# A fused decay attention and mixture of experts: GpSimd decays the next chunk's queries right behind the recall, ahead of the decay of the state

## The chip, the cores and the metric

One core of one Trainium2 chip runs the kernel. The metric is the device time of one execution in microseconds (us); less is better. The engines are TensorE (PE, with its weight loads as PEld), VectorE (DVE), ScalarE (ACT), GpSimd (POOL) and SyncE (SP), which here issues nearly all transfers between HBM and SBUF.

## What is computed

For 4 sequences of 768 positions, 8 heads and head size 64, all in float32, an attention with decay and no softmax, in blocks of 64 positions:

```
intra = einsum('bhic,bhjc->bhij', qb, kb) * Dmask      # lam ** (i - j), 0 above the diagonal
intra = einsum('bhij,bhjd->bhid', intra, vb)
inter = einsum('bhid,bhde->bhie', qb * lam_pow, kv_state)
out[block] = intra + inter
kv_state = lam_block * kv_state + einsum('bhsd,bhse->bhde', kb * rev_pow, vb)
```

The output, as 3072 rows of 512, goes through a soft mixture of 8 experts with 4 slots each: logits `x @ phi`, a softmax over all rows that fills the 32 slots, two matrix products per expert with a relu between them, and a softmax over the slots that hands the result back to the rows.

## The kernel before

The kernel takes blocks of 128 positions instead of 64, which gives 6 chunks for each sequence and T = 24 chunks in all, numbered t = 0 to 23. A chunk holds all 8 heads, two to each of four pairs. The loop over the chunks (from line 532 on) does the attention of one chunk a turn and, every four chunks, a step of the softmax over the rows. Behind the loop come the experts: the two products with w1 and w2, and the rows of the output. The weights are loaded all along, between the chunks' queries, keys and values.

Every engine runs its instructions in the order in which the program issues them: the helper class `InOrder` (its line 63 is the one that all rows of the profile name) keeps that order on each engine. So the order of the calls in the loop is the order of each engine's queue. The parts of a turn that matter here are these.

- `scores(t)`: PE multiplies keys and queries into two PSUM banks (tile sc). In chunks 0 and 1 and in every fourth chunk the scores are made whole, in the others the blocks above the diagonal are left out. `masks(t)`: DVE multiplies them with the powers of lam (tile at).
- `recall(t)`: PE multiplies the state st with the decayed queries qs of this chunk into the banks xa and xb. A chunk that opens a sequence (t = 0, 6, 12, 18) has no recall.
- `attend(t)`: PE adds the product of at and the values to the same banks, the half xa first, then xb; ACT copies them to xt.
- `state(t)`: PE multiplies the decayed keys kd and the values (bank kv), and DVE adds the decayed old state dec to make the new st. In odd chunks and in those that open a sequence this comes right behind the recall, ahead of `attend(t)`; in the other even chunks behind `attend(t)`. The last chunk of a sequence has none.
- POOL's part are three multiplications: `decay_q(t)` makes qs from the loaded queries and the powers qpow (128x512), `decay_k(t)` makes kd from the keys (128x512; in odd chunks from kn, the keys that PE turned and ACT copied), `decay_state(t)` makes dec from st (128x256). Each of qs, kd and dec has one buffer: the next qs can be written only when the recall that reads the old one is done. In chunk 2 POOL also copies phi and blk.
- In even chunks PE also turns the next chunk's keys (tile kv from ident and ld) and two finished chunks (tr, dp) behind the recall.

`decay_q(t + 1)` stands behind `attend(t)`. So in odd chunks and in those that open a sequence POOL's queue reads dec of chunk t, qs of chunk t + 1, kd of chunk t + 1; in the other even chunks it reads qs of t + 1, kd of t + 1, dec of t. No DMA is issued by POOL.

Of the kernel before, what the change touches and what calls it, by code (L numbers as in the profile page):

```python
# [68 lines left out]
def decay_attn_soft_moe(  # L69
# [23 lines left out]
    def bank(tag):  # L93
        return ps.tile([P, 512], F32, tag=tag, name=tag)
# [10 lines left out]
    def load_chunk(t, which=(0, 1, 2, 3)):  # L105
        srcs = (qT, kT, vN, kN)
        for i in which:
            if i == 3 and not loaded(t):
                continue
            tl = loads.tile([P, 512], F32, tag="ld", name="ld")  # L110
            sp.dma_start(out=tl, in_=srcs[i][t])
            IN[t, i] = tl
# [15 lines left out]
    def load_one(pool_, tag, bufs, n=1):  # L128

        t_ = pool_.tile([P, n, 512], F32, tag=tag, name="w2t", bufs=bufs)  # L130
        for m in range(n):
            Q, x, q, i = single.pop()
            sp.dma_start(out=t_[:, m], in_=rows(Q, x, q)[i])
            wt["w2", Q, q, x, i] = t_[:, m]
# [27 lines left out]
    def load_early(n):  # L162
        for _ in range(n):
            if early:
                Q, kk, q = early.pop()
                t_ = slabs.tile([P, 2, 1024], F32, tag="slab", name="slab")
                src = w1[4 * Q + q].rearrange("k p n f -> (k p n f)").rearrange("(p n y) -> n p y", p=P, n=2)
                sp.dma_start(out=t_.rearrange("p i f -> p (i f)"), in_=src[kk])
                wt["w1", Q, q, kk] = t_
            else:  # L170
                load_two()
# [83 lines left out]
    def scores(t):  # L255
        q_, k_ = IN[t, 0], IN[t, 1]
        if t < 2:
            SC["banks"] = [bank(x) for x in (("gl", "dp") if t == 0 else ("sc0", "sc1"))]
        banks = SC["banks"]

        if whole(t):
            for hp in range(HP):
                for hh in range(2):
                    r = slice(64 * hh, 64 * hh + 64)
                    pe.matmul(
                        out=banks[hh][:, hp * P:(hp + 1) * P],
                        lhsT=k_[r, hp * P:(hp + 1) * P],
                        rhs=q_[r, hp * P:(hp + 1) * P],
                        start=True,
                        stop=True,  # L270
                    )
            SC[t] = banks
            return
        for hp in (0, 2, 1, 3):
            for col in (1, 0):

                j = col if plain(hp) else 1 - col
                x = hp * P + 64 * j
                for hh in range(2):
                    r = slice(64 * hh, 64 * hh + 64)  # L280
                    pe.matmul(
                        out=banks[hh][64 * col:64 * col + 64, x:(hp + 1) * P],
                        lhsT=k_[r, hp * P + 64 * j:hp * P + 64 * j + 64],
                        rhs=q_[r, x:(hp + 1) * P],
                        start=True,
                        stop=True,
                    )
        SC[t] = banks
# [15 lines left out]
    def decay_q(t):  # L304
        if t < T and t % NB > 0:
            qs = work.tile([P, HP, P], F32, tag="qs", name="qs")
            pool.tensor_tensor(out=qs, in0=IN[t, 0].rearrange("p (a b) -> p a b", a=HP), in1=qpow, op=ALU.mult)
            QS[t] = qs

    def turn_k(t, tag="kv"):  # L310

        if t < T and t % NB < NB - 1 and not loaded(t):
            tk = bank(tag)
            for hp in range(HP):
                pe.transpose(tk[:, hp * P:(hp + 1) * P], IN[t, 1][:, hp * P:(hp + 1) * P], ident)
            kn = work.tile([P, D], F32, tag="kn", name="kn")
            act.copy(out=kn, in_=tk)
            IN[t, 3] = kn
# [15 lines left out]
    def place(t, hh, hp):  # L334

        g, a = divmod(hp, 2)
        return XB[t][hh][64 * a:64 * a + 64, g * P:(g + 1) * P]

    def recall(t):
        XB[t] = [bank("xa"), bank("xb")]  # L340
        if t % NB > 0:

            qs, st = QS.pop(t), ST["st"]
            for hp in range(HP):
                for hh in range(2):
                    r = slice(64 * hh, 64 * hh + 64)
                    pe.matmul(
                        out=place(t, hh, hp),
                        lhsT=st[r, hp, :],
                        rhs=qs[r, hp, :],  # L350
                        start=(hp < 2),
                        stop=True,
                        skip_group_check=True,
                    )
# [177 lines left out]
    for t in range(T):  # L532
        if t + 2 < T:
            load_chunk(t + 2, (0, 1))

        want = min(NSLAB, max(0, (t * PACE + AHEAD) // 100))
        load_early(want - sent)
        sent = max(sent, want)
        if t + 2 < T:
            load_chunk(t + 2, (2, 3))  # L540
        if t == 0:
            sp.dma_start(out=L, in_=phi.rearrange("p a s -> p (a s)"))

        for _ in range((2, 4, 3)[t - T + 3] if t >= T - 3 else 0):
            load_one(*ld1)
        if t == T - 1:
            load_one(work, "kd", 1)
            load_one(work, "kn", 1)
        last = t == T - 1

        asks = t // 4 - 1 if t > 0 and t % 4 == 0 else G - 1 if last else None
        sums = t // 4 - 1 if t > 4 and t % 4 == 1 else None
        if t == 0:
            turn_k(0, "tr")
            scores(0)
            scores(1)
            turn_v(0)
        elif t > 1:
            scores(t)
        masks(t)  # L560
        if last:
            ask = logits(asks)
            next(ask)

        if t % 4 == 3 or t % 4 == 0:
            next(sm, None)
        if t == T - 1:
            next(sm, None)
        opens = t % NB == 0
        if t == 0:  # L570
            decay_k(0)
            decay_q(1)
        recall(t)
        if sums is not None:
            sm = slot_softmax(sums, weights())
        if t % 2 == 0 and t > 0:
            turn_k(t + 1)
            natural(t - 2)
            natural(t - 1, "dp")
        if sums is not None:  # L580
            next(sm)
        if asks is not None and not last:
            ask = logits(asks)
            next(ask)
        if last:
            natural(t - 1)
            next(ask)
            weights(raw=False)

            phi4 = work.tile([P, HP, 4, SL], F32, tag="carry", name="phi4")  # L590
            four = phi_sb.rearrange("p (a o) s -> p a o s", o=1)
            pool.tensor_copy(out=phi4, in_=four.broadcast_to([P, HP, 4, SL]))
        if opens or t % 2 == 1:

            state(t)
            decay_state(t)
            if t == 0:
                turn_k(1, "tr")
        attend(t)
        if last:  # L600
            cm = bank("kv")
            pe.matmul(out=cm[:, 0:4], lhsT=blk_, rhs=gm, start=True, stop=True)
            dve.tensor_reduce(out=own, in_=cm[:, 0:4], axis=AX.X, op=ALU.min)
        if t == 1:
            powers_of(range(HP, HP + 2), d)
            dve.tensor_reduce(out=sel, in_=ident.rearrange("p (g s) -> p s g", g=4), axis=AX.X, op=ALU.add)
            for n in range(4):
                own_ = bass.AP(
                    tensor=ident.tensor,
                    offset=ident.offset + 16 * (n // 2) + NR * (n % 2),  # L610
                    ap=[ident.ap[0], [64, 2], [40, 2], [1, NR]],
                )
                dve.tensor_reduce(out=own4[:, n:n + 1], in_=own_, axis=AX.XYZ, op=ALU.add)
            dve.tensor_reduce(out=gsel, in_=ident.rearrange("p (g s) -> p g s", g=4), axis=AX.X, op=ALU.add)
        if t > 0:
            decay_q(t + 1)
        if not opens and t % 2 == 0:
            state(t)
        decay_k(t + 1)
        if not opens and t % 2 == 0:  # L620
            decay_state(t)
        if asks is not None and not last:
            next(ask)
        if sums is not None:
            slots(sums)
        if t == 2:
            place_phi()
        if t == 2:
            pool.tensor_copy(out=blk, in_=sel.rearrange("p (o s) -> p o s", o=1).broadcast_to([P, 4, SL]))
# [309 lines left out]
```

## Time and profile before

| | |
|---|---|
| time, median of 3 runs | 169.1 us (168.83 to 170.04) |
| the profiled execution | 169.32 us, its span 167.5 us |
| PE busy | 144.2 us (86%) |
| PEld, DVE, ACT, POOL busy | 104.3, 88.9, 69.1, 70.8 us |
| SP's DMA queue | 61.68 MB, 97.0% of 16 engines' span |
| moved over the span | mean 370 GB/s |

Times in the profile are counted from the start of the span. The chunk loop lies in about the first 113 us, the experts and the output behind it. A row of a timeline gives start, duration, engine, operation, output <- inputs, shapes, and in brackets how long the engine was idle ahead of it and what ended that. PE's matmuls are pipelined and their ends are modelled, so starts are compared and not ends. A wait is put down to what came last by the profile.

### The profile page before, as it was taken

To read this page: it belongs to the slowest core of one execution; us is meant where nothing else is said; L and a number is where in the kernel's file an instruction comes from. 1 tells how busy PE (TensorE), PEld (TensorE's weight loads), DVE (VectorE), ACT (ScalarE), POOL (GpSimd) and SP (SyncE) were. 2 spreads that over 40 slices of the span, in tenths; PEclk is the share of its full clock that TensorE was granted. 3 is DMA by queue.
4 is the path that set the end of the run, shared out by engine and by line. 5 is a ranking of instruction groups with operands and counts; after the bars stand their busy time and mean duration, and the time that the engine had idled before them with its cause. 6 is when DMAs were issued, how large, how long until landed. Compare 5 with 4: busy or idle time off the path is not lost. (4 is left out here: it accounts for less than half of the span.)

```text
span 167.5 us, 6063 instructions
## 1 busy us (share of the span) xinstructions
PE 144.2 (86%) x2531; PEld 104.3 (62%) x2531; DVE 88.9 (53%) x208; ACT 69.1 (41%) x174; POOL 70.8 (42%) x102
## 2 busy tenths in 40 slices
PE   6697879997899998997989789899899999997700
PEld 6576768686785786696858678586333365564600
DVE  3949661745475546634674447556437690243900
ACT  3133714572345544461647234554104650343800
POOL 2868494226638306857313663920000698000000
PEclk9999999999999999999999999999999999999975
DMA  5999999999999999999999989998999999998797
GB/s 167 322 416 407 403 394 378 405 397 412 380 394 374 345 351 401 412 423 377 346 400 406 401 311 367 370 366 294 337 399 420 420 417 416 403 363 288 275 412 253
DMA packets 26891, 62.07 MB, mean 370 GB/s; under 512 B 2672, under 2 KB 7408, under 8 KB 24816
## 3 DMA queue, kind: packets, MB, share of 16 engines
q1 hardware_dynamic: 26720, 61.68, 97.0%
q8 instruction: 20, 0.33, 0.7%
q14 instruction: 7, 0.06, 0.1%
q10 hardware_dynamic: 144, 0.01, 0.1%
HBM read 55.38 MB, written 6.29 MB: 368 GB/s over the span
## 5 line engine op out<-in xcount | busy, mean ns | idle before, releaser
L63 DVE TENSOR_TENSOR at<-sc,mask 128x512 f32<-128x512 f32 x46 | 29.6, 685 | 14.8 <-PE sc L63 13.6
L63 PE MATMUL sc<-ld 64*64 64x128 f32 (+2 forms) x640 | 23.4, 256 | 3.3 <-issue 1.7
L63 POOL TENSOR_TENSOR qs<-ld,qpow 128x512 f32<-128x512 f32 x20 | 25.8, 1290 | 0.1
L63 PEld LDWEIGHTS sc<-ld 64*64 64x64 f32 (+1 forms) x640 | 19.3, 141 | 10.3 <-issue 3.8
L63 POOL TENSOR_TENSOR dec<-st,qpow 128x256 f32<-128x256 f32 x16 | 10.0, 626 | 30.0 <-DVE st L63 12.8
L63 POOL CAST ct<-part 32x256 fp32r<-32x256 f32 x26 | 10.3, 397 | 22.2 <-DVE part L63 21.1
L63 PE MATMUL xa<-qs,st 64*64 64x128 f32 x160 | 13.6, 281 | 5.2 <-POOL qs L63 5.1
L63 DVE TENSOR_TENSOR st<-dec,kv 128x256 f32<-128x256 f32 x16 | 6.7, 418 | 14.3 <-PE kv L63 14.3
L63 ACT COPY xt<-xa 128x256 f32<-128x256 f32 x24 | 8.8, 367 | 13.2 <-PE xa L63 13.2
L63 POOL TENSOR_TENSOR kd<-ld,kpow 128x512 f32<-128x512 f32 x11 | 11.6, 1055 | 6.0 <-DMA ld<-kN 3.9
L63 ACT COPY vs<-ld 64x256 f32<-64x256 f32 x34 | 13.7, 403 | 0.8
L63 PE MATMUL kv<-ld,kd 128*64 128x64 f32 x320 | 13.3, 225 | 0.7 <-POOL kd L63 0.7
L63 POOL TENSOR_TENSOR kd<-kn,kpow 128x512 f32<-128x512 f32 x9 | 9.4, 1046 | 9.4 <-ACT xt L63 5.2
L63 PE MATMUL xb<-qs,st 64*64 64x128 f32 x160 | 13.2, 281 | 0.0
L63 PEld LDWEIGHTS kv<-ld,kd 128*64 128x64 f32 x320 | 11.4, 137 | 2.9 <-POOL kd L63 1.7
L63 PEld LDWEIGHTS xa<-qs,st 64*64 64x64 f32 x160 | 8.8, 132 | 7.0 <-POOL qs L63 6.2
L63 PE MATMUL xa<-at,ld 128*64 128x128 f32 x124 | 11.5, 284 | 1.4 <-DVE at L63 1.4
L63 ACT COPY x<-tr 128x512 f32<-128x512 f32 (+1 forms) x13 | 7.4, 571 | 10.1 <-PE tr L63 10.0
L63 PE MATMUL xb<-at,ld 128*64 128x128 f32 x124 | 11.1, 277 | 0.0
L63 ACT COPY xt<-xb 128x256 f32<-128x256 f32 x23 | 8.6, 375 | 1.2 <-PE xb L63 0.5
L63 ACT COPY kn<-kv 128x512 f32<-128x512 f32 x7 | 4.1, 587 | 11.8 <-PE kv L63 11.8
L63 ACT ACTIVATE ce<-ce 128x128 f32<-128x128 f32 x6 | 1.9, 310 | 17.2 <-DVE ce L63 17.2
(151 smaller groups left out, 278.2 us busy)
## 6 DMA issues: line engine op xcount, KB each, us to landing
slab<-w_x SPq DMA_DIRECT2D x16, 1024.0 KB, 7.4
w2p<-w_x SPq DMA_DIRECT2D x9, 1024.0 KB, 11.4
w2t<-w_x SPq DMA_DIRECT2D x28, 256.0 KB, 5.3
ld<-qT SPq DMA_DIRECT2D x24, 256.0 KB, 6.9
ld<-kT SPq DMA_DIRECT2D x24, 256.0 KB, 5.3
ld<-vN SPq DMA_DIRECT2D x24, 256.0 KB, 6.9
y<-o SPq DMA_DIRECT2D x18, 256.0 KB, 3.5
ld<-kN SPq DMA_DIRECT2D x11, 256.0 KB, 7.2
```

Of the source, the lines that this page charges most:

```text
L63: return self._tc.keep_in_program_order(f(*args, **kwargs))
```

## The change

`decay_q(t + 1)` moves from behind `attend(t)` to right behind `recall(t)`. Where `decay_state(t)` stands between the two places, qs of chunk t + 1 now comes ahead of dec of chunk t in POOL's queue: in the odd chunks 1, 3, 7, 9, 13, 15, 19 and 21 and in the chunks 6, 12 and 18. Nothing else is changed.

```
         recall(t)
+        if t > 0:
+            decay_q(t + 1)
         if sums is not None:
             sm = slot_softmax(sums, weights())
...
             dve.tensor_reduce(out=gsel, in_=ident.rearrange("p (g s) -> p g s", g=4), axis=AX.X, op=ALU.add)
-        if t > 0:
-            decay_q(t + 1)
         if not opens and t % 2 == 0:
             state(t)
         decay_k(t + 1)
```

On POOL, from chunk 3 to the middle of chunk 8, the queue of before reads as follows (dec, qs and kd with the number of their tile; ld are loaded queries or keys, kn turned keys; the first row is the dec of chunk 3, the sixth that of chunk 6, the ninth that of chunk 7):

```order
L63 TENSOR_TENSOR dec_420<-st_196,qpow_123 128x256
L63 TENSOR_TENSOR qs_432<-ld_280,qpow_123 128x512
L63 TENSOR_TENSOR kd_434<-ld_288,kpow_132 128x512
L63 TENSOR_TENSOR qs_516<-ld_374,qpow_123 128x512
L63 TENSOR_TENSOR kd_589<-ld_444,kpow_132 128x512
L63 TENSOR_TENSOR dec_660<-st_196,qpow_123 128x256
L63 TENSOR_TENSOR qs_674<-ld_529,qpow_123 128x512
L63 TENSOR_TENSOR kd_676<-kn_634,kpow_132 128x512
L63 TENSOR_TENSOR dec_727<-st_196,qpow_123 128x256
L63 TENSOR_TENSOR qs_739<-ld_597,qpow_123 128x512
L63 TENSOR_TENSOR kd_741<-ld_605,kpow_132 128x512
L63 TENSOR_TENSOR qs_834<-ld_678,qpow_123 128x512
```

In these twelve places dec comes first, then qs and kd of the next chunk. The same stretch of the changed kernel:

```order
L63 TENSOR_TENSOR qs_410<-ld_280,qpow_123 128x512
L63 TENSOR_TENSOR dec_422<-st_196,qpow_123 128x256
L63 TENSOR_TENSOR kd_434<-ld_288,kpow_132 128x512
L63 TENSOR_TENSOR qs_468<-ld_374,qpow_123 128x512
L63 TENSOR_TENSOR kd_589<-ld_444,kpow_132 128x512
L63 TENSOR_TENSOR qs_629<-ld_529,qpow_123 128x512
L63 TENSOR_TENSOR dec_662<-st_196,qpow_123 128x256
L63 TENSOR_TENSOR kd_676<-kn_636,kpow_132 128x512
L63 TENSOR_TENSOR qs_717<-ld_597,qpow_123 128x512
L63 TENSOR_TENSOR dec_729<-st_196,qpow_123 128x256
L63 TENSOR_TENSOR kd_741<-ld_605,kpow_132 128x512
L63 TENSOR_TENSOR qs_776<-ld_678,qpow_123 128x512
```

The three dec have moved one place back, behind the qs of the next chunk; kd has kept its place, behind both.

## Rows read from the trace of the kernel before

**Rows 1.** The page: the span, and each engine's busy time, share and instructions.
```profile
span 167.5 us, 6063 instructions
PE 144.2 (86%) x2531; PEld 104.3 (62%) x2531; DVE 88.9 (53%) x208; ACT 69.1 (41%) x174; POOL 70.8 (42%) x102
```

**Rows 2.** Waits of PEld from 8 to 113 us: total us, times, longest us.
```profile
PEld xa L63 <- POOL qs L63: 6.2, 7, 1.2
...
PEld kv L63 <- POOL kd L63: 1.7, 5, 0.6
```

**Rows 3.** Timeline of PEld in chunks 7 and 8: start us, us, instructions, idle before.
```profile
36.71 0.76 PEld L63 LDWEIGHTS sc<-ld 64*64 64x64 f32 x32 [0.17 <-issue]
38.37 0.13 PEld L63 LDWEIGHTS xa<-qs,st 64*64 64x64 f32 x1 [0.90 <-POOL qs L63]
...
39.37 0.55 PEld L63 LDWEIGHTS kv<-ld,kd 128*64 128x64 f32 x16 [0.58 <-POOL kd L63]
...
40.22 0.25 PEld L63 LDWEIGHTS xb<-at,ld 128*64 128x64 f32 x4
...
42.58 0.13 PEld L63 LDWEIGHTS xa<-qs,st 64*64 64x64 f32 x1 [0.74 <-POOL qs L63]
...
43.17 0.42 PEld L63 LDWEIGHTS kv<-ident,ld 128*128 128x128 f32 x4 [0.17 <-issue]
```

**Rows 4.** Timeline of POOL in chunks 6 and 7.
```profile
36.46 0.62 POOL L63 TENSOR_TENSOR dec<-st,qpow 128x256 f32<-128x256 f32 x1 [6.14 <-DVE st L63]
37.04 1.28 POOL L63 TENSOR_TENSOR qs<-ld,qpow 128x512 f32<-128x512 f32 x1
38.27 1.05 POOL L63 TENSOR_TENSOR kd<-kn,kpow 128x512 f32<-128x512 f32 x1
40.67 0.62 POOL L63 TENSOR_TENSOR dec<-st,qpow 128x256 f32<-128x256 f32 x1 [1.36 <-DVE st L63]
```

**Rows 5.** Timeline of PEld: first load of the recalls of chunks 4 and 22.
```profile
24.93 0.13 PEld L63 LDWEIGHTS xa<-qs,st 64*64 64x64 f32 x1 [1.24 <-POOL qs L63]
...
106.95 0.13 PEld L63 LDWEIGHTS xa<-qs,st 64*64 64x64 f32 x1 [0.58 <-POOL qs L63]
```

**Rows 6.** Timelines of DVE and PEld around chunk 2: scans, recall, attention.
```profile
13.20 3.57 DVE L63 TENSOR_TENSOR_SCAN mask<-lam_sb,d 128x128 f32<-128x128 f32 x4
...
15.42 0.13 PEld L63 LDWEIGHTS xa<-qs,st 64*64 64x64 f32 x1 [1.11 <-POOL qs L63]
...
18.19 0.20 PEld L63 LDWEIGHTS xa<-at,ld 128*64 128x64 f32 x4 [0.88 <-DVE at L63]
```

**Rows 7.** Timeline of PE in chunk 11: its scores and the start of its recall.
```profile
55.79 0.90 PE L63 MATMUL sc<-ld 64*64 64x64 f32 x32
56.55 0.29 PE L63 MATMUL xa<-qs,st 64*64 64x128 f32 x1
```

**Rows 8.** Timeline of POOL at the end of chunk 2 and in chunk 3.
```profile
22.78 0.29 POOL L63 COPY blk<-sel 128x128 f32<-128x128 f32 x1
23.04 0.62 POOL L63 TENSOR_TENSOR dec<-st,qpow 128x256 f32<-128x256 f32 x1
23.62 1.26 POOL L63 TENSOR_TENSOR qs<-ld,qpow 128x512 f32<-128x512 f32 x1
```

**Rows 9.** Timeline of DVE: the masked scores of chunk 7.
```profile
37.66 1.29 DVE L63 TENSOR_TENSOR at<-sc,mask 128x512 f32<-128x512 f32 x2 [1.29 <-PE sc L63]
```

**Rows 10.** Timeline of PEld: first and last of three stops inside the scores.
```profile
52.24 0.53 PEld L63 LDWEIGHTS sc<-ld 64*64 64x64 f32 x19 [0.59 <-issue]
...
78.01 0.52 PEld L63 LDWEIGHTS sc<-ld 64*128 64x128 f32 x6 [1.11 <-issue]
```

**Rows 11.** The page, DMA queues: packets, MB, share of 16 engines.
```profile
q8 instruction: 20, 0.33, 0.7%
```

**Rows 12.** The tile w2p from 122 to 152 us: its DMA issues, their landing.
```profile
L63 SPq DMA_DIRECT2D w2p<-w_x x8: 367/374/677, 123.5 to 133.2; - x8
...
DMA to landing us min/median/max: 7.8/11.7/15.8
```

**Rows 13.** Timeline of PE: the last matmuls that read w2p.
```profile
149.85 1.93 PE L63 MATMUL xa<-w2p,hz 128*32 128x256 f32 x32
```

More of the change, by code (lines that the diff above doesn't have):

```diff
@@ L573, in decay_attn_soft_moe @@
         recall(t)
+        if t > 0:
+            decay_q(t + 1)
         if sums is not None:
@@ L614, in decay_attn_soft_moe @@
             dve.tensor_reduce(out=gsel, in_=ident.rearrange("p (g s) -> p g s", g=4), axis=AX.X, op=ALU.add)
-        if t > 0:
-            decay_q(t + 1)
         if not opens and t % 2 == 0:
```

## The prediction, made before the result was known

> **What bounds the kernel now.** The waits of the weight-load queue come first, because matmuls and their weight loads are issued by one sequencer and fill most of the span [rows 1]. Of all waits that another engine causes on it in the chunk loop, the largest is the one for qs, the decayed queries that GpSimd (POOL) writes: 6.2 us in seven waits; kd, the decayed keys, adds 1.7 us in five [rows 2]. No transfer comes near that. So the loop is set by TensorE (PE), and where PE stands still longest it stands for POOL.
>
> The timelines of PEld and POOL then show why. In chunk 7 the scores' weights start at 36.71 and the first load of the recall at 38.37, after 0.90 us of waiting for qs; then 0.58 us go to kd before the state at 39.37; in chunk 8 the recall waits 0.74 us more [rows 3]. POOL in the same time: dec of chunk 6 from 36.46, when st of chunk 6 is there, qs of chunk 7 from 37.04 to 38.32, kd of chunk 7 from 38.27 to 39.32 [rows 4]. PE starts 0.05 us after each of them. POOL stood idle for 6.14 us ahead of that dec and for 1.36 us ahead of the next [rows 4], with qs queued behind: an idle engine in front of the operation that PE waits for. That the queries have long been loaded follows from the same rows, since qs starts the moment dec ends.
>
> The seven waits are in the recalls of chunks 2 (1.11 us), 4 (1.24), 7 (0.90), 8 (0.74), 19 (0.90, the row of chunk 7 again), 20 (0.74, the row of chunk 8 again) and 22 (0.58) [rows 3, 5, 6]; they sum to the 6.2.
>
> **The change part by part.** No instruction is added or taken away; on PE, VectorE (DVE), ScalarE and SP the order is the same, no DMA issue is moved, and POOL's own queue holds no DMA. On POOL eleven qs change places with one dec: in odd chunks that decay a state, and in the chunks 6, 12 and 18 that open a sequence. In the other even chunks qs was ahead already and nothing is moved.
>
> *The opening chunks (6 and 18).* qs of chunk 7 needs only its queries and the recall of chunk 5, so it runs inside POOL's idle 6.14 us and is free. dec keeps its start at 36.46, which st sets. kd follows at 37.04 in place of 38.27 and ends 1.05 later, at 38.09. Without the wait the recall starts as far behind the scores as in chunk 11, where nothing holds it: 56.55 - 55.79 = 0.76 [rows 7], so at 37.47. The next kind of matmul follows a recall after 0.59 us (42.58 to 43.17) [rows 3]: 38.06. kd is there at 38.09 + 0.05 = 38.14. The state starts at 38.14 in place of 39.37: **1.23 us** off chunk 7, and again off chunk 19, whose row reads the same.
>
> *The odd chunks.* qs of chunk 8 now starts when the recall of chunk 7 is done and kd has left POOL, 38.3, and takes 1.28 as chunk 7's does [rows 4]: done near 39.6. Without its wait, and with the 1.23 us, the recall of chunk 8 starts at 42.58 - 0.74 - 1.23 = 40.61. It is covered by the state, the attention and the scores on PE by 1.0 us, so the **0.74 us** of chunk 8 go, and of chunk 20 too; by the same reading the **0.58 us** of chunk 22.
>
> In chunk 4 POOL is busy in one piece until 23.04 with copies of phi; qs starts there in place of 23.62 [rows 8], **0.58 us** earlier, and the rest of its 1.24 us stays.
>
> *Chunk 2 gives nothing.* Its 1.11 us of waiting go, but the attention behind it waits 0.88 us for DVE's masked scores at 18.19, and DVE is held by four scans from 13.20 that take 3.57 us [rows 6]. PE arrives earlier and waits longer. If the scans end earlier because POOL's operations fall otherwise among them, up to 1.11 us come out; I take 0 and keep 1.11 for the low end. On this the Trainium skill, "SBUF — State Buffer", section "SBUF: two separate sides", says that a VectorE operation with two SBUF inputs and a GpSimd operation exclude each other for the whole instruction. The scans' long durations here agree with it; the sum by it would lie between the two ends just given.
>
> *What becomes later.* dec of an odd chunk starts behind qs: in chunk 7 about 0.1 us later against st than now. Its reader is st of the next chunk, behind that chunk's attention: several us of cover, cost 0. kd in an odd chunk comes about 1 us earlier, cost 0. DVE's masked scores become the next to be late: the second half is done at 37.66 + 1.29 = 38.95 [rows 9]; the second half of chunk 7's attention comes 40.22 - 39.37 = 0.85 us behind the state's start [rows 3], 38.14 + 0.85 = 38.99. It just fits; priced at 0, with 0.1 us each in two chunks as the other end.
>
> *Chunks 10, 13, 14 and 16* get the same swap or stand behind one, and I give them nothing: PE does not wait for qs there by the rows. In the scores of three of them the loads stop for a reason that the profile calls issue, 0.59 us at 52.24 in chunk 10 and 1.11 us at 78.01 in chunk 16 [rows 10], and the qs wait lies under that.
>
> **Sum**, against the profiled execution (169.32 us, its span 167.5 [rows 1] and 1.8 around it): 0.58 + 1.23 + 0.74 + 1.23 + 0.74 + 0.58 = 5.10 us. From that I take one more stall of the size at 52.24, 0.59 us, since PE calls for instructions and data faster than now: 4.5 us. The median of the runs is 0.2 us below the profiled one: 169.1 - 4.5 = **164.6**.
>
> What those stalls are the rows don't say outright. 20 packets of 16 KB came over the instruction queue [rows 11], so fetching is what I suspect: the blocks share the DMA engines with the loads and can be late. The Trainium skill, "Runtime: NRT & Kernel Launch", section "Instruction fetch mechanics", says that a fetch of 16 KiB (256 instructions) runs while the page before it executes and is mostly hidden. The size agrees with the packets; the stalls speak against "hidden" when the DMA engines are full. By the page alone the deduction would be 0 and the time 164.0.
>
> **The rivals.**
> 1. *The stalls take back a part.* For it: the DMA queue is at work through the whole loop, and the stretch from 52 to 78 holds three stalls, so PE may be held there by something that doesn't care about qs. If PE's lead on reaching 78 us is lost, the 0.58, 1.23 and 0.74 of chunks 4 to 8 go and 2.55 us stay: 166.6. Against it: the stalls sit at fixed places and were paid for already.
> 2. *The weights behind the loop don't come earlier.* The last w2 tile is issued at 133.2 and lands after 15.8 us, at 149.0 [rows 12]; the last 32 matmuls start at 149.85 and take 1.93, and the tile's half of them starts 0.97 later [rows 13]. If the landing can't move at all, only 150.8 - 149.0 = 1.8 us can be gained: 167.3. Against it: the issues in that stretch hang on tiles that PE and POOL release, and these come earlier too.
> 3. *It does nothing:* the recall waits for something that ends as late as qs. st is the only other input; in chunk 7 it was there before dec began, at 36.46. Time 169.1.
> 4. *Slower:* a faster PE runs into a late instruction block at each of the 20 blocks and no longer at three. A gain of 5.1 us is gone at 0.26 us for each, and slower by over 1% (1.7 us) from 0.34 us; at the 0.59 us of chunk 10 for each it is 11.8 - 5.1 = 6.7 us slower, 175.8. Against it: the time between two blocks shrinks by a few per cent only, and most blocks show no stall now.
>
> **How the numbers follow.** Main case 0.62 (163.3 to 165.9: the sum without deduction and chunk 2 partly gained, or two stalls more), rival 1 0.16, rival 2 0.08, rival 3 0.07, rival 4 0.04, and 0.03 for more than all terms. The low end is 169.1 - 5.10 - 1.11 = 162.9; the high end takes in rivals 1 and 2: 167.4. What is left out is 0.14. Faster by over 1%, which is about what a measurement of this kernel can tell from no change, means below 167.4: main case, rival 1, the 0.03 and half of rival 2, 0.85. Within 1%: rival 3 and the other half, 0.11. Slower: 0.04.
>
> **What would show it.** In the profile after, the wait of the recall for qs should fall from 6.2 us to about 0.7 (chunk 4 alone), and the wait of the state for kd by about 1 us. POOL should show qs directly ahead of the dec of chunk 6, long before st. Chunk 2's attention should wait about 2 us for DVE. The sum is wrong if the idle before the recalls has moved to stalls called issue (rival 1 or 4), to the second half of the attention (DVE), or to waits for w2 tiles late in the span (rival 2); it is wrong at the root if the recalls of chunks 7 and 8 start no earlier behind their scores.

## The result, and the profile after

The changed kernel takes 163.96 us (median of 5 runs, 162.82 to 167.32), the kernel before 168.85 us in the same comparison (168.17 to 170.04): a ratio of 0.9665, 95% interval 0.9598 to 0.9732. The ratios and their intervals, here and below, count only the executions of a kernel that lie within 1.5% of its fastest, so that this one leaves out those of 166.45 and 167.32 us. Forecast were 164.6 us in a range of 162.9 to 167.4. The profiled execution of the changed kernel is its longest (167.32 us), so most of the reading below is done in a second profile of the same kernel, unedited, called *again* (164.15 us).

The page of the changed kernel and then of *again*, the lines that answer to [rows 1]:

```profile
span 165.5 us, 6063 instructions
PE 146.0 (88%) x2531; PEld 106.4 (64%) x2531; DVE 91.7 (55%) x208; ACT 69.4 (42%) x174; POOL 70.9 (43%) x102
```

```profile
span 162.4 us, 6063 instructions
PE 144.5 (89%) x2531; PEld 105.5 (65%) x2531; DVE 91.3 (56%) x208; ACT 69.0 (43%) x174; POOL 70.9 (44%) x102
```

The work is the same; PE is busier because the span is shorter. The waits of PEld from 8 to 113 us in *again* (total us, times, longest us) answer to [rows 2]:

```profile
PEld xa L63 <- DVE at L63: 3.5, 6, 2.3
PEld xa L63 <- issue: 2.8, 9, 1.1
PEld sc L63 <- DMA ld<-vN: 2.5, 3, 0.8
...
PEld sc L63 <- issue: 2.0, 6, 1.1
...
PEld kv L63 <- POOL kd L63: 0.9, 4, 0.3
...
PEld xb L63 <- DVE at L63: 0.5, 3, 0.2
```

The row that led before, the wait for qs of 6.2 us, is gone altogether, and kd has fallen from 1.7 to 0.9 us. What leads now is one long wait for DVE's masked scores and two stops that end for a reason called issue; these are what is left to explain. The three idle times of 0.84 us put down to loads are none of it: one of that length stands ahead of the scores of chunks 6, 10, 14, 18 and 22 in the kernel before too, put down to a load in one profile and to issue in another.

Chunks 7 and 8 on PEld in *again* (start us, us, instructions, idle before), against [rows 3]:

```profile
36.80 0.76 PEld L63 LDWEIGHTS sc<-ld 64*64 64x64 f32 x32 [0.17 <-issue]
37.42 0.13 PEld L63 LDWEIGHTS xa<-qs,st 64*64 64x64 f32 x1
...
38.39 0.55 PEld L63 LDWEIGHTS kv<-ld,kd 128*64 128x64 f32 x16 [0.17 <-POOL kd L63]
...
39.88 0.97 PEld L63 LDWEIGHTS sc<-ld 64*128 64x128 f32 x16 [0.17 <-DMA ld<-qT]
40.97 0.13 PEld L63 LDWEIGHTS xa<-qs,st 64*64 64x64 f32 x1
```

In the kernel before, the scores of chunk 8 start here:

```profile
40.86 0.97 PEld L63 LDWEIGHTS sc<-ld 64*128 64x128 f32 x16 [0.17 <-DMA ld<-qT]
```

The recall of chunk 7 starts 0.62 us behind its scores in place of 1.66, the state 1.59 in place of 2.66; the recall of chunk 8 follows its scores by 1.09 in place of 1.72 (40.86 to 42.58), and neither recall has a wait. POOL in *again*, against [rows 4]:

```profile
30.71 1.27 POOL L63 TENSOR_TENSOR qs<-ld,qpow 128x512 f32<-128x512 f32 x1 [0.32 <-POOL kd L63]
36.54 0.62 POOL L63 TENSOR_TENSOR dec<-st,qpow 128x256 f32<-128x256 f32 x1 [4.55 <-DVE st L63]
37.12 1.05 POOL L63 TENSOR_TENSOR kd<-kn,kpow 128x512 f32<-128x512 f32 x1
38.60 1.27 POOL L63 TENSOR_TENSOR qs<-ld,qpow 128x512 f32<-128x512 f32 x1 [0.43 <-POOL kd L63]
```

qs of chunk 7 runs at 30.71, long before st lets dec go at 36.54; it costs nothing there, as forecast.

Where the 5.17 us between the two profiled executions (169.32 and 164.15) come from can be read chunk by chunk: each value is by how much the start of the attention's first load has moved against the other kernel, less what it had moved one row earlier. The second pair of kernels is explained below; in it no stop called issue stands inside the scores, recalls or attentions of the loop. Each column rests on one execution of each kernel.

| chunk | forecast, us | *again* against before | the pair with few loads |
|---|---|---|---|
| start of the loop | 0 | 0.46 | -0.19 |
| 2 to 4 | 0.58 | -0.54 | -0.55 |
| 7 | 1.23 | 1.06 | 1.23 |
| 8 | 0.74 | 0.62 | 0.62 |
| 10 | 0 | 0.67 | 0.55 |
| 11, 12 | 0 | -1.15 | 0 |
| 13 | 0 | 1.02 | 1.02 |
| 14 | 0 | 0.19 | 0.05 |
| 16 | 0 | 0 | 1.17 |
| 17, 18 | 0 | 0.31 | 0 |
| 19 | 1.23 | 1.24 | 1.24 |
| 20 | 0.74 | 0.62 | 0.62 |
| 22 | 0.58 | 0.67 | 0.67 |
| one more stop | -0.59 | (in the rows) | |
| sum | 4.5 | 5.17 | 6.43 |

The forecast chunks 7, 8, 19, 20 and 22 give 4.21 of the 4.52 us put on them. But chunks 2 to 4 lose where 0.58 was expected, and chunks 10, 13 and 14 give 1.88 us that were put at nothing. The sum was nearly right because these errors cancel, which is luck.

### The profile page after: what moved, and what is told of

Its sections match the earlier page's. It is cut to its first block, busy times and chain, and to the rows that moved or that the text cites. A ratio compares the mean times of both kernels' runs of the same rounds, so it can differ in the third digit from the quotient of the medians.

```text
span 165.5 us, 6063 instructions
## 1 busy us (share of the span) xinstructions
PE 146.0 (88%) x2531; PEld 106.4 (64%) x2531; DVE 91.7 (55%) x208; ACT 69.4 (42%) x174; POOL 70.9 (43%) x102
## 4 chain that ended last, share of the span: by engine, by line
PE 78%; DVE 6%; DMA 4%; issue 4%; SPq 1%; ACT 1%; DVEq 0%; ACTq 0%
PE xa L63 20%; PE sc L63 14%; PE kv L63 14%; PE xb L63 11%; PE gl L63 9%; PE tr L63 6%; PE dp L63 5%; DMA ld<-kT 3%; DVE o L63 2%; DVE mask L63 2%; DMA y<-o 1%; DVE at L63 1%; SPq L63 1%; DVE acc L63 0%; DVEq L935 0%
## 5 line engine op out<-in xcount | busy, mean ns | idle before, releaser
L63 PE MATMUL sc<-ld 64*64 64x128 f32 (+2 forms) x640 | 24.0, 262 | 2.4 <-issue 1.7
L63 PEld LDWEIGHTS sc<-ld 64*64 64x64 f32 (+1 forms) x640 | 20.1, 146 | 9.3 <-issue 3.2
L63 PE MATMUL xa<-at,ld 128*64 128x128 f32 x124 | 12.0, 284 | 2.7 <-DVE at L63 2.3
L63 PE MATMUL xb<-qs,st 64*64 64x128 f32 x160 | 13.8, 285 | 0.3 <-issue 0.3
L63 PE MATMUL kv<-ld,kd 128*64 128x64 f32 x320 | 13.8, 230 | 0.1
L63 PEld LDWEIGHTS xa<-qs,st 64*64 64x64 f32 x160 | 9.3, 137 | 1.5 <-issue 1.0
L63 PEld LDWEIGHTS xa<-at,ld 128*64 128x64 f32 x124 | 6.6, 137 | 5.3 <-DVE at L63 3.3
L63 PEld LDWEIGHTS xb<-qs,st 64*64 64x64 f32 x160 | 9.2, 137 | 0.8 <-issue 0.6
```

The costliest lines, as they stand in the source:

```text
L63: return self._tc.keep_in_program_order(f(*args, **kwargs))
```

## The experiments

### The same kernel again

*Again* was run beside the three kernels of the next section, on the same chip.

> The changed kernel once more, unedited, for its spread and for a second profile. In the first profile of it TensorE's granted clock fell to half from 20.1 to 23.5 us, right behind a stop of 2.3 us ahead of chunk 2's attention, and chunk 4's attention came at 28.2 us, 0.6 us later than before the change. Theory (the stop that the change lengthens calls the half clock in some executions): times fall into two groups, about 163 and about 166 us; in a profile without the half clock in the loop chunk 4's attention starts near 27.0 us and the span is about 161 us. Rival (the clock has nothing to do with it, late instruction blocks scatter the time): the span varies by 2 us or more with the same clock in the loop.

Measured: 163.89 us (163.28 to 170.02), ratio 0.9696 [0.9644, 0.9747]. The two groups of times that were expected don't show: five of the six executions lie between 163.28 and 164.70 us. TensorE's granted clock falls in its loop too. In chunk 2 the rows of *again* are, first of PEld and then of DVE, against [rows 6]:

```profile
13.71 0.13 PEld L63 LDWEIGHTS xa<-qs,st 64*64 64x64 f32 x1
...
17.94 0.20 PEld L63 LDWEIGHTS xa<-at,ld 128*64 128x64 f32 x4 [2.30 <-DVE at L63]
...
23.92 0.75 PEld L63 LDWEIGHTS sc<-ld 64*128 64x128 f32 x12 [0.17 <-issue]
```

```profile
12.73 3.80 DVE L63 TENSOR_TENSOR_SCAN mask<-lam_sb,d 128x128 f32<-128x128 f32 x4
16.46 0.34 DVE L63 TENSOR_REDUCE sel<-ident 128x32 f32<-128x128 f32 x1
16.72 0.38 DVE L63 TENSOR_REDUCE own<-ident 128x1 f32<-128x16 f32 x4
17.02 0.27 DVE L63 TENSOR_REDUCE gsel<-ident 128x4 f32<-128x128 f32 x1
17.21 1.28 DVE L63 TENSOR_TENSOR at<-sc,mask 128x512 f32<-128x512 f32 x2
```

The recall has come 1.71 us earlier (15.42 before) and the attention only 0.25: PE waits 2.30 us in place of 0.88, for four scans and six reductions that stand ahead of the masked scores on DVE. That was forecast. What was not is the granted clock behind it (columns: stretch, length, busy time and instructions of PE, PEld, DVE, ACT and POOL, granted clock, DMA share, GB/s), in *again* and then in the kernel before, in about the same place:

```profile
18.73:22.15 3.42, 3.42 (x68) 3.30 (x70) 0.65 (x2) 1.47 (x4) 1.59 (x3) 0.50 1.06 406
```

```profile
18.70:22.10 3.40, 3.40 (x100) 3.05 (x96) 1.76 (x5) 1.55 (x4) 1.96 (x4) 1.00 1.05 403
```

The clock is at 0.50, the level of 1.2 GHz, from 18.73 to 22.15, where the kernel before has 1.00, that of 2.4 GHz. From the attention of chunk 2 to the scores of chunk 4 it takes 23.92 - 17.94 = 5.98 us; the kernel before takes 4.54 (18.19 [rows 6] to 22.73):

```profile
22.73 0.86 PEld L63 LDWEIGHTS sc<-ld 64*128 64x128 f32 x14 [0.17 <-DMA ld<-qT]
```

So the swap of chunk 1, which can bring nothing in chunk 2, costs 1.44 us here; part of it is hidden under the wait for qs that chunk 4 would otherwise still have. The Trainium skill, "TensorE: Matmul & The Clock Gate", section "Part 1: The HAM clock gate", says that the throttled clock is the default and that activity releases it; that the clock falls behind PE's longest standstill of the loop agrees with it. Why it doesn't fall behind the same standstill in *odd_only* (below) is not answered by that.

### The swap everywhere but in chunk 1 (*not1*), in the opening chunks alone (*open_only*), in the odd chunks alone (*odd_only*)

All three are the changed kernel with this edit, the condition being `t > 1` in *not1*, `opens and t > 0` in *open_only* and `t % 2 == 1` in *odd_only*:

```
         recall(t)
-        if t > 0:
+        early_q = t > 1
+        if early_q:
             decay_q(t + 1)
...
             dve.tensor_reduce(out=gsel, in_=ident.rearrange("p (g s) -> p g s", g=4), axis=AX.X, op=ALU.add)
+        if t > 0 and not early_q:
+            decay_q(t + 1)
```

> The change everywhere but in chunk 1, where the decay of the state stays ahead of the queries. Theory: the stop ahead of chunk 2's attention is 0.9 us as before the change and not 2.3 us, the granted clock stays at 1.00 until the tail, and every execution comes to 163 to 164 us: median as the better executions of the changed kernel, spread under 1 us. Rival (the scatter comes from late instruction blocks): the same two groups as the changed kernel, 163 and 166 us.

> The queries ahead of the decay in the opening chunks 6, 12 and 18 alone. By the sum of the prediction 1.23 us each in chunks 7 and 19: 2.5 us, 166.4 us against 168.9. Rival (TensorE is paced by late instruction blocks, so that what one place gains is lost at the next block): 0.5 to 1.5 us.

> The queries ahead of the decay in the odd chunks alone. By the sum 0.58 + 0.74 + 0.74 + 0.58 = 2.6 us: 166.2 us against 168.9, with chunk 2's recall 1.1 us earlier and its attention not. Rival (late instruction blocks): 0.5 to 1.5 us. Rival (the longer stop in chunk 2 calls the half clock): some executions come 1.7 us later than the others, at 168 us.

| | median, us | lowest to highest | ratio to before, 95% |
|---|---|---|---|
| before (11 runs) | 168.77 | 167.83 to 170.52 | 1 |
| *again* | 163.89 | 163.28 to 170.02 | 0.9696 [0.9644, 0.9747] |
| *not1* | 162.72 | 161.63 to 162.86 | 0.9612 [0.9565, 0.9659] |
| *open_only* | 167.08 | 165.99 to 170.87 | 0.9872 [0.9819, 0.9924] |
| *odd_only* | 165.71 | 164.26 to 166.62 | 0.9787 [0.9729, 0.9846] |

Without the swap of chunk 1 the kernel is 1.17 us faster than with all swaps by the medians, and somewhat faster than was expected (163 to 164). In its profile PEld waits in xa from 8 to 113 us as follows:

```profile
PEld xa L63 <- DVE at L63: 1.9, 5, 0.9
...
PEld xa L63 <- POOL qs L63: 1.8, 2, 1.1
```

The wait for DVE is back at 0.9 us at most, the one for qs in chunk 2 is back too, the clock stays at 1.00 through the loop, and chunk 4 has gained 0.58 us, the forecast term to the digit (its wait for qs is 0.65 where [rows 5] have 1.24). Between *again* and *not1* chunks 2 to 4 differ by 0.54 + 0.58 = 1.12 us, close to the 1.17 us of the medians; that the two agree so well is in part luck, because by chunk 23 the two profiles are 2.48 us apart, and that of *not1* is its fastest execution (161.63). So the swap of chunk 1 takes time where all others give some, by a way that the forecast did not have. The two halves bring 1.7 and 3.1 us by the medians (2.5 and 2.6 were expected), 4.8 together where the whole brings 4.9. By the ratios the halves would be 2.2 and 3.6 us, with half-widths of 0.9 and 1.0 us, so the agreement of the sums proves little. Chunk by chunk the parts do not simply add up: in *open_only* chunks 7, 13 and 19 gain 1.24, 1.01 and 1.24 us, but chunks 8 and 20 lose 0.52 each, because there qs still stands behind dec and its wait grows (1.27 us in chunk 8 in place of 0.74). Only both halves together keep the gain of chunk 7 and add that of chunk 8.

### Few loads in the loop, without and with the change (*light_before*, *light_after*)

Both kernels load about half as many slabs of w1 during the loop and the rest behind it; the computation is complete. The whole time therefore can't be compared with the others, the loops of the two can be compared with each other.

```
-PACE = 76
+PACE = 38
...
             pool.tensor_copy(out=blk, in_=sel.rearrange("p (o s) -> p o s", o=1).broadcast_to([P, 4, SL]))
+    load_early(NSLAB - sent)
     load_one(work, "mask", 1, 3)
```

> The kernel before with half as many weight slabs loaded during the chunk loop; the others are loaded behind it, so that the whole takes longer and only the loop is compared. Theory (instruction blocks for TensorE come late because they queue behind the loads): the stops called issue inside the scores of chunks 10, 13 and 16 (0.59, 0.62 and 1.11 us) vanish, and the wait of the recall for qs shows in their place: from 6.2 us in 7 waits to 8 us or more in 9 or 10. Rival (the stops belong to the instructions and not to the transfers): they stay, and the waits for qs stay at 6.2 us.

> The same thinning of the slabs in the changed kernel. Theory: no stops called issue above 0.3 us, no waits for qs but chunk 4's, and chunk 23's recall starts 7 to 8 us earlier than in the thinned kernel before (5.1 by the sum, 2 to 3 in chunks 10, 13, 14 and 16 that the stops had hidden), or 1.7 less if the half clock falls on it. Rival (the stops stay): 4 to 5 us, as in the two kernels with all slabs.

Measured: 187.46 and 179.25 us, one execution each. The stops called issue in the kernels with all loads first, in *again*, in chunks 11 and 16 (the timeline of PEld):

```profile
56.54 0.13 PEld L63 LDWEIGHTS xa<-at,ld 128*64 128x64 f32 x1 [1.13 <-issue]
...
75.68 0.52 PEld L63 LDWEIGHTS sc<-ld 64*128 64x128 f32 x6 [1.11 <-issue]
```

and in the first profile of the changed kernel, in chunks 10 and 11:

```profile
51.97 0.46 PEld L63 LDWEIGHTS sc<-ld 64*64 64x64 f32 x18 [1.01 <-issue]
...
57.97 0.13 PEld L63 LDWEIGHTS xa<-at,ld 128*64 128x64 f32 x1 [0.57 <-issue]
```

They answer to [rows 10], but the two executions have them in different chunks and sizes; only that of chunk 16 is in both and in before, 1.11 us, and there it swallows the whole gain of that chunk. With few loads in the loop no such stop is left. From 24 us to the loop's end one idle time of 0.4 us or more in *light_after* is called issue, ahead of the first load of chunk 22's scores; *light_before* has the same there and one more ahead of chunk 14's (68.38). These are the idle times of 0.84 us named above; none lies inside scores, recall or attention:

```profile
98.66 0.76 PEld L63 LDWEIGHTS sc<-ld 64*64 64x64 f32 x32 [0.84 <-issue]
```

```profile
104.42 0.76 PEld L63 LDWEIGHTS sc<-ld 64*64 64x64 f32 x32 [0.84 <-issue]
```

And in *light_before*, where the kernel before shows stops inside the scores of chunks 10, 13 and 16, the recalls of these chunks wait for qs openly (the whole row of waits, from 8 to 113 us, and the timeline of PEld):

```profile
PEld xa L63 <- POOL qs L63: 9.0, 10, 1.3
```

```profile
52.19 0.13 PEld L63 LDWEIGHTS xa<-qs,st 64*64 64x64 f32 x1 [0.58 <-POOL qs L63]
...
64.89 0.13 PEld L63 LDWEIGHTS xa<-qs,st 64*64 64x64 f32 x1 [0.89 <-POOL qs L63]
...
77.80 0.13 PEld L63 LDWEIGHTS xa<-qs,st 64*64 64x64 f32 x1 [1.30 <-POOL qs L63]
```

Ten waits of 9.0 us in place of seven of 6.2, and *light_after* has none. So the swap is worth these three chunks as well, 2.74 us by the third column of the table, wherever no stop stands in the way. Few loads are not needed for that: *open_only*, with all loads, has no such stop in its loop either, and its recalls of chunks 10 and 16, whose qs still stands behind a dec, wait as long as those of *light_before*:

```profile
51.60 0.13 PEld L63 LDWEIGHTS xa<-qs,st 64*64 64x64 f32 x1 [0.58 <-POOL qs L63]
...
76.63 0.13 PEld L63 LDWEIGHTS xa<-qs,st 64*64 64x64 f32 x1 [1.30 <-POOL qs L63]
```

So what is moved during the loop does not decide alone on the stops. From 46 to 78 us it is 402 GB/s in the changed kernel and 318 in *light_after* (both below), but 387 in *open_only*, with none, and 385 in the kernel before, with three.

What the stops are can be read from the kept traces, which hold every packet of the instruction queue q8 [rows 11] with its time. If all instructions of TensorE, weight loads and matmuls together, are numbered from 0 in the order of their starts, the stops stand at fixed places: the thirteen profiles of this study have 26 stops of 0.40 us or more that lie inside scores, recalls or attentions and are called issue, and the number of the first load behind each of them leaves 193 or 194 when divided by 256. And each ends 1.26 to 1.60 us after a packet of 16384 bytes on q8 has ended. In the kernel before and in *again*:

| stop | packet on q8 ends, us | next load starts, us | stop, us |
|---|---|---|---|
| before, chunk 10 | 50.81 | 52.24 | 0.59 |
| before, chunk 13 | 63.54 | 64.88 | 0.62 |
| before, chunk 16 | 76.65 | 78.01 | 1.11 |
| *again*, chunk 11 | 55.12 | 56.54 | 1.13 |
| *again*, chunk 16 | 74.23 | 75.68 | 1.11 |

The idle times of 0.84 us lie at none of these places. So the stops are late instruction blocks, as the prediction suspected. Their places are the same in all kernels; at which of them PE stops is decided by whether the block is there when PE comes. At the 14 such places between 24 and 113 us the last packet on q8 had ended 2 us or more before in 13 cases in *light_after*, in 12 in *open_only* and in 6 in *again*. What delays a block in one execution and not in the other is not settled by this.

The windows from 46 to 78 us, of the changed kernel and of *light_after* (columns as above):

```profile
46.00:78.00 32.00, 29.54 (x629) 23.68 (x626) 18.06 (x42) 15.86 (x44) 18.05 (x19) 1.00 1.02 402
```

```profile
46.00:78.00 32.00, 31.72 (x690) 25.79 (x682) 19.96 (x47) 16.62 (x45) 19.45 (x20) 1.00 0.92 318
```

In the same 32 us PE does 690 matmuls in place of 629, with the same program; but *not1*, which moves 410 GB/s there, does 683.

### Room for chunk 4 (*not1_phi*)

*not1* with the copies of phi behind `decay_q(3)` in chunk 2, ahead of the state, and that of blk in chunk 5, so that qs of chunk 4 doesn't stand behind them [rows 8].

```
+        if t == 2:
+            place_phi()
         if not opens and t % 2 == 0:
             state(t)
...
-        if t == 2:
-            place_phi()
-        if t == 2:
+        if t == 5:
             pool.tensor_copy(out=blk, in_=sel.rearrange("p (o s) -> p o s", o=1).broadcast_to([P, 4, SL]))
```

> The change everywhere but in chunk 1, and POOL's copies of phi moved from the end of chunk 2 to behind the queries of chunk 3, into idle time; the copy of blk moved to chunk 5. Theory: the rest of chunk 4's wait for qs (1.1 us of PEld in the run without the change in chunk 1) goes: 0.6 to 1.1 us less than that run, 161.6 to 162.2 us. Rival (instruction blocks take it back): no difference, 162.7 us.

Measured: 162.51 us (162.10 to 163.26), ratio 0.9625 [0.9593, 0.9657]. The recall of chunk 4 gains 0.54 us more than in *not1* against its own chunk 2, of the 0.65 that were left there (the 1.1 us of the expectation are chunk 2's wait); but a stop of 1.11 us is back in chunk 16, where *not1* has none, and by the last chunk *not1_phi* is 0.69 us behind. So in these two profiles the gain was taken back, as rival 1 had it. They exaggerate it, because that of *not1* is its fastest execution; by the medians *not1_phi* is 0.21 us faster, within the noise, where 0.6 to 1.1 was expected.

### The standstill of chunk 2 removed at its source (*best3*)

The changed kernel with all swaps, with *not1_phi*'s moves on POOL, and on DVE: two of the four scans in chunk 0, the reductions behind the masked scores of chunk 2.

```
-        if t == 1:
-            powers_of(range(HP, HP + 2), d)
+        if t < 2:
+            powers_of([HP + t], d)
+        if t == 2:
+            place_phi()
+        if not opens and t % 2 == 0:
+            state(t)
+        decay_k(t + 1)
+        if not opens and t % 2 == 0:
+            decay_state(t)
+        if t == 2:
             dve.tensor_reduce(out=sel, in_=ident.rearrange("p (g s) -> p s g", g=4), axis=AX.X, op=ALU.add)
```

> The change everywhere, the copies of phi and blk moved as in the run beside it, and DVE's work ahead of chunk 2 thinned: two of its four scans moved to chunk 0, its reductions (sel, own4, gsel) behind chunk 2's masked scores. Theory (DVE's chain makes chunk 2's stop, the stop calls the half clock): chunk 2's attention waits under 0.5 us for DVE, starts at 16.5 us or before against 17.9, the granted clock stays 1.00 until the tail in every execution; chunk 4 gains about 1 us more from phi: 160 to 161 us. Rival (instruction blocks or loads take it back): 162 to 163 us.

Measured: 162.07 us (161.28 to 164.02), ratio 0.9581 [0.9549, 0.9612]: the fastest kernel of this study, though its interval and that of *not1* overlap. Its attention of chunk 2, and its scores of chunk 16:

```profile
15.87 0.20 PEld L63 LDWEIGHTS xa<-at,ld 128*64 128x64 f32 x4 [0.17 <-issue]
...
72.80 0.52 PEld L63 LDWEIGHTS sc<-ld 64*128 64x128 f32 x6 [0.83 <-issue]
```

The wait for DVE is gone as expected, but the time missed the expected 160 to 161 us and came out as the rival had it. The attention of chunk 2 starts 1.88 us earlier than in *not1* (17.75), and the clock stays at 1.00. By chunk 16 the lead is used up, by two stops (0.57 us in chunk 11 and 0.83 in chunk 16) and by losses of 0.25 to 0.32 us in five other chunks, and in chunk 23 *best3* is 0.09 us behind *not1* (105.98 and 105.89). Its windows show what the loop runs into (GB/s last):

```profile
8.00:46.00 38.00, 37.79 (x788) 30.77 (x790) 24.44 (x57) 18.67 (x49) 25.26 (x30) 1.00 1.04 412
46.00:78.00 32.00, 30.59 (x638) 24.55 (x634) 17.97 (x40) 16.35 (x45) 16.72 (x17) 1.00 1.03 408
78.00:109.00 31.00, 30.46 (x618) 23.94 (x607) 20.26 (x53) 15.58 (x42) 14.42 (x15) 1.00 1.03 405
```

PE is busy for 37.79 of the first 38 us shown and for 1.4 us less than the whole of the next 32, while the transfers run at 405 to 412 GB/s throughout. That this rate is what calls the stops is not shown: *not1* moves 404 to 410 GB/s in the same stretches and has one stop, of 0.86 us in chunk 17.

### Smaller transfers (*split*)

*best3* with each 1 MB slab of w1 issued as two transfers of half the size, to see whether the stops come from large transfers ahead in the queue.

```
-                sp.dma_start(out=t_.rearrange("p i f -> p (i f)"), in_=src[kk])
+                for i in range(2):
+                    sp.dma_start(out=t_[:, i], in_=src[kk][:, 1024 * i:1024 * i + 1024])
```

> The run with the thinned DVE work (best3) with each slab of w1 loaded by two transfers of 0.5 MB in place of one of 1 MB, the same bytes. At most eight transfers are under way, so fewer bytes lie ahead of an instruction block. Theory (blocks come late by what lies ahead of them in the DMA queue): the stops called issue get shorter, chunk 23's attention comes 1 to 2 us earlier than in best3, 160.5 to 161.5 us. Rival (the loop is at the rate of the DMA engines, 410 GB/s, and the bytes decide): as best3, 162 us.

Measured: 163.01 us (162.58 to 164.94), ratio 0.9678 [0.9627, 0.9729]. The late blocks stop PE for 1.22 us at 62.55 and 0.83 at 75.33, no less than in *best3* (0.57, 0.83 and 0.47), and two loads of keys are late as well (1.60 us at 39.77; 1.27 at 56.84, which the row of PEld calls issue and that of PE names). So neither the time nor this one profile bears out the theory that the size of one transfer delays the blocks.

### The swap of chunk 1 alone (*only1*), and a standstill without any swap (*stop_before*)

*only1* is the changed kernel with `early_q = t == 1` in the edit above. *stop_before* is the kernel before with one reduction done six times, which holds DVE, and so PE in chunk 2, without touching POOL's order.

```
-            dve.tensor_reduce(out=gsel, in_=ident.rearrange("p (g s) -> p g s", g=4), axis=AX.X, op=ALU.add)
+            for _ in range(6):
+                dve.tensor_reduce(out=gsel, in_=ident.rearrange("p (g s) -> p g s", g=4), axis=AX.X, op=ALU.add)
```

> The queries ahead of the decay in chunk 1 alone; everything else as before the change. Theory (the swap there only lengthens chunk 2's stop from 0.88 to 2.3 us, and that calls the half clock in some executions): no gain, 168.9 us, and where the half clock falls, chunk 4's attention comes 1 to 1.8 us later than before and the time is about 170 us. Rival (chunk 1's swap is harmless): the same times as before and the clock at 1.00 until the tail.

> The kernel before, with the last of DVE's reductions ahead of chunk 2's masked scores made six times: chunk 2's stop for DVE grows from 0.88 to about 2 us without any swap. Theory (it is the stop that calls the half clock): the granted clock falls to half behind chunk 2 in some executions, which then cost 1.7 us on top of the 1.0 to 1.4 us of the reductions. Rival (the swap itself, or GpSimd's work at that place, calls it): 1.0 to 1.4 us later, 170.1 us, and the clock at 1.00.

Measured: *only1* 169.68 us (168.51 to 173.02, 12 runs), ratio 1.0028 [0.9992, 1.0065]; *stop_before* 171.06 us (169.63 to 175.99, 12 runs), ratio 1.0113 [1.0079, 1.0148]. The attention of chunk 2 in *only1*, in *stop_before* and in *odd_only* (the timeline of PEld):

```profile
18.05 0.24 PEld L63 LDWEIGHTS xa<-at,ld 128*64 128x64 f32 x4 [2.30 <-DVE at L63]
```

```profile
19.43 0.20 PEld L63 LDWEIGHTS xa<-at,ld 128*64 128x64 f32 x4 [2.49 <-DVE at L63]
```

```profile
17.92 0.20 PEld L63 LDWEIGHTS xa<-at,ld 128*64 128x64 f32 x4 [2.30 <-DVE at L63]
```

In *only1* the clock falls behind it and chunk 4's attention is 0.89 us later than before, so the swap alone brings nothing or a little loss. In *stop_before* the stop is the longest of all and the clock stays at 1.00 behind it, in the one execution that has a profile:

```profile
19.40:22.80 3.40, 3.37 (x92) 2.95 (x94) 1.76 (x4) 1.55 (x4) 1.47 (x2) 1.00 0.82 313
```

*odd_only* has the stop of 2.30 us and the full clock as well. It has the same swaps in chunks 1 and 3 as *again*, and over chunks 2 to 4 it gains 0.37 us where *again* loses 0.54: 0.91 us go with the clock. The other 0.21 us to the 0.58 of *not1* go with the longer standstill itself. Of the six profiles in which PE stands 2.30 us or more in chunk 2, four show the clock at 0.50 behind it (the changed kernel twice, *light_after*, *only1*); none of the other seven does. So the fall comes with the long standstill, but not each time, and what decides it between two executions stays open. In the profile of *stop_before* the standstill costs 1.23 us by the recall of chunk 4 [rows 5] (26.16 against 24.93). By the medians the kernel is 2.11 us slower than before, and the profiled execution (169.80 us) is the second fastest of the twelve: it and the fastest have a mean granted clock of 0.980 and 0.982, the other ten 0.979 or less and 170.21 us or more. So the clock may have fallen in some of those; no profile of them shows it.

## Why the prediction was right, and where it was not

**The mechanism: right.** PE waited for qs, and qs stood behind a dec that st held. With the order changed the wait for qs goes from 6.2 us to none, and the terms of chunks 7 and 19 are 1.23 and 1.24 us in the pair with few loads (1.06 and 1.24 in *again*), 1.23 forecast. The recall of chunk 7 follows its scores by 0.62 us where 0.76 was taken, which doesn't enter the sum, since kd sets the start of the state. Chunks 8 and 20 give 0.62 where 0.74 was read off the wait: the recall follows the scores by 1.09 us without any wait, where 1.72 - 0.74 = 0.98 was taken, so 0.12 us of what the row calls a wait is a gap that stays without one: in *again* the scores' loads end at 40.85 and the recall starts at 40.97. Chunk 22 gives 0.67, 0.58 forecast.

**Chunk 2 gives nothing: right as to the gain, wrong as to the price.** The step said that PE arrives earlier and waits longer, and left it at nothing. The standstill did become 2.30 us ("about 2 us" was forecast), but the clock fell to 1.2 GHz behind it, and chunks 2 to 4 lost 0.54 us where 0.58 was to be gained, 0.91 of the difference with the clock and 0.21 with the longer standstill. A standstill that moved was priced by its own length; what comes behind it on the same engine was not asked. The scans, which by the step could also have ended earlier, took 3.80 us in place of 3.57, so the end of that range at nothing held.

**Chunks 10, 13, 14 and 16 at nothing: wrong.** The step read that PE doesn't wait for qs there, because the trace puts those rows down to issue. A stop had only covered the wait: of the two the later shows, and where the block is there in time, in *light_before* and *open_only*, the wait shows. Without stops the chunks are worth 0.55, 1.02, 0.05 and 1.17 us; in *again* the first three came out as 0.67, 1.02 and 0.19, and that of chunk 16 stayed under its stop. This is the largest term that the sum missed.

**One more stop, 0.59 us: the suspicion right, the count not.** What was suspected, late instruction blocks, is what the stops are. But their number is no term that can be added: in *again* chunks 11 and 12 lost 1.15 us to a stop of 1.13 that the kernel before doesn't have, and the 0.59 and 0.62 us of chunks 10 and 13 were gone, two stops in place of three. In the first profile of the changed kernel there are six between 0.48 and 1.11 us, with 3.5 us in xa and 3.2 in sc that are called issue (rows below), and its last chunk is only 2.03 us ahead of before. Its waits of PEld from 8 to 113 us:

```profile
PEld xa L63 <- issue: 3.5, 11, 0.8
...
PEld sc L63 <- issue: 3.2, 8, 1.1
```

On the cause, the prediction set the stops against the Trainium skill, "Runtime: NRT & Kernel Launch", section "Instruction fetch mechanics", which calls the fetch mostly hidden. The trace agrees in part: at most places no stop shows, but at up to six in one loop the fetch is not hidden, for 0.40 to 1.38 us.

**The sum.** For *again*: chunks 7, 8, 19, 20 and 22 gave 4.21, chunks 10, 13 and 14 gave 1.88, chunks 17 and 18 gave 0.31 (which was not followed further), the start of the loop 0.46; chunks 2 to 4 took 0.54, the stop 1.15. That is 5.17 us, where 5.10 - 0.59 was forecast. The number was right, three of its terms were not; that they cancel was not foreseen.

**What was put at nothing.** dec later and kd earlier cost nothing that can be seen: the wait for kd fell by 0.8 us (about 1 us was forecast), and the second half of the attention waits for DVE three times (four before), 0.2 us at most. That it "just fits" held.

**The rivals.** Rival 1 (the stops take back a part) took place: in *again* with one new stop, in the first profile nearly in full, where the lead is 0.40 us in chunk 16 and 2.03 at the end (2.55 by the rival; the clock had a part in it, with 0.62 us lost by chunk 4). What it held against itself, that the stops sit at fixed places and were paid for, is half right: the places are fixed, but PE stops now at one and now at another. Rival 2 (the last w2 tiles don't come earlier) did not: *again* is 5.17 us ahead in chunk 23 and its span is 5.1 us shorter, *not1* 7.65 and 7.7; what is won in the loop reaches the end. Rival 3 did not come about. Of rival 4 the way did, late blocks at more places than three in the first profile, but not the size: the kernel is faster. A swap that makes a place slower by itself, chunk 1's, was in none of them.

## What to carry to other kernels

When an operation that waits long stands in a queue ahead of one that could run, look who waits for the second: the gain is the whole distance, also at places where the trace names another cause, because a row names only the later of two. Where an edit lets an engine reach a fixed obstacle earlier and gain nothing there, leave that place out of the edit or remove the obstacle: here a longer standstill of TensorE was followed by half its clock more often than not. And where instruction blocks can come late, count the places where a stop can stand and not only those where one stood: here there is one every 256 instructions of TensorE, and what two further edits won early in the loop was used up, in the profiles, by stops and small losses later in it.

## What was not expected of the hardware

The granted clock fell to 0.50 in the middle of an execution in which PE is busy for 89% of the span, behind one standstill of 2.30 us, in four of the six profiles with a standstill of that length or more; in *again* the next 4.54 us of work then took 5.98. The stops called issue, 0.40 to 1.38 us each, all stand at the same step of 256 instructions, 1.26 to 1.60 us behind a packet of the instruction queue, and two executions of the same kernel stop at different ones of these places. They were gone with half the slabs out of the loop (318 GB/s), and in one kernel with all of them in it (387 GB/s). Halving the transfers' size did not shorten them.
